# Attention and gated MLP on one core: batch 1 loaded in chunks, its k turned by DMA, and a new order for the opening

## The chip, the core and the metric

The kernel runs on one core of a Trainium2 chip. The metric is device time in microseconds (us): 309.43 us is the median of the three runs shown (308.65 to 309.45). A profile is one further execution in which every engine's instructions are recorded. A core has TensorE (PE), VectorE (DVE), ScalarE (ACT), GpSimd (POOL) and SyncE (SP), each with a queue of its own, and DMA queues that are fed here by POOL and SyncE.

## The reference

```python
B, H, S, D = 8, 8, 576, 64
scores = scale * np.matmul(q, k.transpose(0, 1, 3, 2))        # scale = 1/sqrt(D)
mask = (rel >= 0) & (rel < 64)                                # rel = row - column
attn = softmax(np.where(mask, scores, -1e9))
x = np.matmul(attn, v).transpose(0, 2, 1, 3).reshape(B * S, H * D)   # 4608 x 512
h = x @ w_in                                                  # 512 x 2048
out = (h * np.cos(h)) @ w_out                                 # 2048 x 512, float32
```

Inputs are float32. Each row of q attends to itself and the 63 rows before it.

## The kernel before, in words

**Attention.** A batch has eight heads, taken as four pairs p; a pair fills 128 partitions (2 x 64). The 576 rows are nine units j of 64 rows; a unit's 64 queries meet the 128 keys of units j - 1 and j. Scores are made in groups of up to four units, listed in `groups`; groups 0 to 7 are units 0 to 7 of batch 0 (group 2p + g is pair p, half g), group 8 is batch 0's last unit, groups 9 to 18 are batch 1. A group goes through `g_scores` (TensorE into a PSUM bank), `g_max` (DVE), `g_exp` (ACT), `g_inv` (DVE), `g_norm` (POOL or DVE, gives w), and `g_trans`, which transposes w by DMA, or on TensorE followed by `g_put` for the groups in `direct`. `values` and `values_half` multiply with v on TensorE, and `put_x` and `put_x_half` copy the result into xT. Odd units need a shifted copy of v, which the `spread_v` steps make.

**q and k.** Scores need q and k with the head dimension on partitions. In batches 0 and 1 `load_heads` (L161) loads a pair of heads in runs of nine rows, TensorE transposes them in 18 pieces of 64x64 per pair and tensor (`transposed`, L209), and `put_q` (L229) or `put_k` (L262) copy them out of PSUM into row order; the two heads of a pair are then multiplied one by one (L309), with lhsT of 64x64. Batches 2 and later use `load_chunk` (L178): 96 rows of all eight heads. Their k is turned by DMA transposes on SyncE (`turn_k`, L259); q is transposed on TensorE in six pieces of 96x128 per pair or turned by DMA, and `put_block` (L238) copies each head of a pair into its own half of a block that is zero elsewhere (`qblocks`), so that one product of 128x128 (L303) makes both heads' scores. `clear_first` (L545) zeroes those blocks.

**MLP.** Tokens go in tiles of 512. Tile 0 (batch 0's first 512 rows) is in the opening: `first_half` (L412; f = 0 to 7, half g) makes two columns of h for 256 tokens, `sine_half` and `gate_half` make the gate, and `second_part` (L431; quarter of d_ff, 128 tokens) sums the output. Tiles 1 to 8 run in the main loop (`first`, L450; L595, L598, L609), with the attention of later batches put between their products by planned times.

**The opening.** It is a hand-listed order, the string `FIRST` (L50 to L72): each word is a step that issues its instructions on its engines' queues at that place, and every engine works its own queue in order. The steps that matter here: `Lq`, `Lk`, `Lv`, `Lwi`, `Lwo` are loads of q, k, v, and quarters of w_in and w_out, nearly all of them on POOL's queue (pair 0 of batch 0 is loaded plain by SyncE and cast by `cq`, `ck`); `io` makes the iotas of the mask on POOL (L143), `mk` and `mc` the mask on DVE and ACT; `tq`, `pq`, `tk`, `pk` transpose and copy q and k of batch 0, `Tq`, `Pq`, `Tk`, `Pk` those of batch 1; `s m e i n w c` are the stages of groups 0 to 7 and `Gs Gm Ge Gi Gn Gw/Gc Gp` those of groups 8 to 18; `zA zB zC` and `yA yB y` spread v; `v x` are values of tile 0, `V X` of tile 1; `h S g` the halves of w_in products, sines and gates, `o oc` the w_out parts and their copies; `ms` are the clears; `tb`, `tb2` load ScalarE's tables. The letter at a step's end names its engine (a ACT, d DVE, p POOL, s SyncE). A load on POOL also waits, in turns of eight completion semaphores, for the load eight places before it.

Of the kernel before, what the change touches and what calls it, by code (L numbers as in the profile page):

```python
# [10 lines left out]
def _safe_warn(msg, *a, **kw):  # L11
# [64 lines left out]
def kernel(  # L76
# [32 lines left out]
    qtiles += [turned[:, p] for p in range(PAIRS)]  # L109
# [99 lines left out]
    def transposed(name, b, p):  # L209
        t_ps = ps_t.tile([128, S], BF16, tag="t", name=f"t{name}_ps")  # L210
        of = st[name, b]
        if b < 2:
            for c in range(RC):
                for h in range(2):
                    d = slice(64 * h, 64 * h + 64)
                    nc.tensor.transpose(t_ps[d, 64 * c:64 * c + 64], of[d, p, 64 * c:64 * c + 64], ident[d, d])
        else:
            for c in range(TURNED.get(b, 0) if name == "q" else 0, NC):
                nc.tensor.transpose(t_ps[:, NP * c:NP * c + NP], of[:, c, 128 * p:128 * p + 128], ident[:NP, :NP])  # L219
        return t_ps  # L220


    def in_order(t_ps, to, b):
        return (t_ps.rearrange("d (c p) -> d p c", c=RC), to.rearrange("d (p c) -> d p c", c=RC)) if b < 2 else (t_ps, to)

    def tr_q(b, p):
        st["tq", b, p] = transposed("q", b, p)

    def put_q(b, p, engine=None):  # L229
        of, to = in_order(st.pop(("tq", b, p)), qtiles[b * PAIRS + p], b)  # L230
        if b:
            copy(engine, to, of)
        elif engine == "a":
            nc.scalar.mul(to, of, scale)
        else:
            nc.vector.tensor_scalar(to, of, scale, None, ALU.mult)

    def put_block(b, p, h):  # L238
        d = slice(64 * h, 64 * h + 64)
        lo = TURNED.get(b, 0) * NP // 64  # L240
        copy("d", qblocks[(b % 2) * PAIRS + p][d, lo:, h], st["tq", b, p][d].rearrange("d (j t) -> d j t", j=NU)[:, lo:])
# [40 lines left out]
    def g_scores(n, which):  # L282
# [13 lines left out]
        for u, (b, p, j) in enumerate(units):  # L296
# [5 lines left out]
            if b > 1:  # L302
# [4 lines left out]
            for h in range(2):  # L307
                d = slice(64 * h, 64 * h + 64)
                nc.tensor.matmul(out=s_ps[d, u, 0:64 * chunks].rearrange("p (a t) -> p a t", a=chunks),  # L309
                                 lhsT=qtiles[b * PAIRS + p][d, 64 * j:64 * j + 64], rhs=rhs[d], start=n >= n_first,  # L310
# [237 lines left out]
    def spread_first(lo, hi):  # L548
# [5 lines left out]
             "Lq1": lambda p: load_heads("q", 1, p, 1), "Lk1": lambda p: load_heads("k", 1, p, 1),  # L554
# [4 lines left out]
             "tq": lambda p: tr_q(0, p), "tk": lambda p: tr_k(0, p), "Tq": lambda p: tr_q(1, p), "Tk": lambda p: tr_k(1, p),  # L559
             "pq": lambda p, engine: put_q(0, p, engine), "pk": lambda p, engine: put_k(0, p, engine),  # L560
             "Pq": lambda p, engine: put_q(1, p, engine), "Pk": lambda p, engine: put_k(1, p, engine),
# [87 lines left out]
```

## Time and profile before

| what | before |
|---|---|
| median of the runs shown | 309.43 us |
| span of the profiled execution | 306.3 us |
| DVE, ACT, POOL busy | 75%, 76%, 63% |
| HBM read, written | 36.70 MB, 9.44 MB |
| DMA packets | 159945, of which 148256 are under 512 B |

The span is from the first to the last instruction of the profiled execution; the runs' times are some 3 us longer. A row of a timeline gives start, duration, engine, line, operation, tiles and count; a row of a group gives its count, then busy time and mean ns of one, then the engine's idle time before it and what ended it. TensorE products are pipelined and their ends are modelled, so the time of one is read from start to start.

### The profile page before, as it was taken

The numbers are of one execution on the slowest core, as the hardware profiler recorded it, in microseconds if no ns is written. First come the engines' busy times: TensorE is split into PE (matmuls) and PEld (weight loads), VectorE is DVE, ScalarE is ACT, GpSimd is POOL, SyncE is SP. The second block draws the span as 40 slices with busy tenths as digits, with TensorE's granted clock in tenths as the row PEclk, the third lists the DMA queues.
The fourth block names the chain that finished last, engine by engine and source line by source line (L and its number), as shares of the span: only waits on it lengthen the run. The fifth ranks groups of instructions, "written<-read, shape, count | busy, mean of one in ns | idle before, by whom it ended". The sixth has DMA issues, their size and how long they took to land.

```text
span 306.3 us, 7904 instructions
## 1 busy us (share of the span) xinstructions
PE 296.2 (97%) x2616; PEld 159.0 (52%) x2616; DVE 228.5 (75%) x908; ACT 234.3 (76%) x785; POOL 192.5 (63%) x228
## 2 busy tenths in 40 slices
PE   3889999999999999999999999999999999999996
PEld 2768844545555555445544555454545554454443
DVE  5999978599769976798579857986698668235801
ACT  5998799677997799779976997699879986116600
POOL 8998579995659669967998599959903930000000
PEclk9999999999999999999999999999999999999999
DMA  7999999999999995999999999999794643011011
GB/s 146 179 212 192 200 180 130 121 149 191 226 113 116 175 223 80 121 133 232 125 121 137 231 143 104 157 221 148 86 137 107 169 78 141 2 68 71 1 67 70
DMA packets 159945, 42.14 MB, mean 138 GB/s; under 512 B 148256, under 2 KB 155168, under 8 KB 159904
## 3 DMA queue, kind: packets, MB, share of 16 engines
q0 software_dynamic: 100192, 18.06, 80.1%
q1 hardware_dynamic: 59568, 23.38, 40.6%
q8 instruction: 20, 0.33, 0.4%
q14 instruction: 21, 0.17, 0.2%
q10 hardware_dynamic: 144, 0.20, 0.2%
HBM read 36.70 MB, written 9.44 MB: 151 GB/s over the span
## 4 chain that ended last, share of the span: by engine, by line
PE 90%; POOL 4%; DMA 2%; DVE 1%; ACT 1%; issue 1%; POOLq 0%; DVEq 0%; ACTq 0%
PE h_ps L453 35%; PE out_ps L609 35%; PE h_ps L417 5%; PE s_ps L303 4%; PE out_ps L436 4%; PE o_ps L384 3%; DMA k<-in_k_dram 2%; POOL w L353 2%; PE tq_ps L219 1%; POOL v L188 1%; PE out_ps L465 1%; PE s_ps L309 1%; PE tw_ps L364 1%; POOL w_in L204 1%; ACT e L336 1%
## 5 line engine op out<-in xcount | busy, mean ns | idle before, releaser
L609 PE MATMUL out_ps<-w_out,gT 128*128 128x512 bf16 x496 | 117.3, 379 | 0.0
L453 PE MATMUL h_ps<-xT,w_in 128*128 128x512 bf16 x512 | 115.3, 379 | 0.3
L595 ACT ACTIVATE sin<-h_ps 128x512 f32<-128x512 f32 x128 | 73.7, 598 | 32.7 <-PE h_ps L453 31.4
L598 DVE TENSOR_TENSOR gT<-h_ps,sin 128x512 bf16<-128x512 f32 x128 | 82.1, 685 | 21.9 <-ACT sin L595 21.2
L336 ACT ACTIVATE e<-s,negm 128x128 f32<-128x128 f32 (+1 forms) x256 | 97.1, 382 | 0.6 <-DVE negm L324 0.6
L353 POOL TENSOR_TENSOR w<-e,rden 128x512 bf16<-128x512 f32 (+1 forms) x74 | 70.0, 962 | 36.6 <-DVE rden L346 18.8
L453 PEld LDWEIGHTS <-w_in 128*128 128x128 bf16 x512 | 48.8, 98 | 54.7 <-issue 0.4
L609 PEld LDWEIGHTS <-gT 128*128 128x128 bf16 x496 | 45.9, 98 | 44.2
L324 DVE CUSTOM_DVE_ANT_0 s<-s_ps,mask 128x128 f32<-128x128 f32 (+1 forms) x256 | 56.4, 279 | 1.7 <-PE s_ps L309 0.9
L336 ACT ACTIVATION_READ_ACCUMULATOR e<-s,negm 128x1 f32 x256 | 48.3, 189 | 0.0
L182 POOL DMA_DIRECT2D q<-in_q_dram x36 | 28.3, 785 | 10.7 <-DMA q<-in_q_dram 4.0
L188 POOL DMA_DIRECT2D v<-in_v_dram x40 | 34.4, 878 | 0.3 <-issue 0.2
L182 POOL DMA_DIRECT2D k<-in_k_dram x36 | 28.2, 783 | 3.9 <-DMA k<-in_k_dram 1.2
L137 ACT COPY out_sb<-out_ps 128x512 f32<-128x512 f32 (+1 forms) x18 | 10.2, 566 | 24.5 <-PE out_ps L609 18.4
L346 DVE RECIPROCAL rden<-den 128x4 f32<-128x4 f32 (+1 forms) x79 | 13.1, 166 | 19.0 <-ACT e L336 18.6
L303 PEld LDWEIGHTS <-qB 128*128 128x128 bf16 x216 | 16.5, 98 | 14.2
L137 DVE CAST xT<-o_ps 128x512 bf16<-128x512 f32 x24 | 15.5, 677 | 10.1 <-PE o_ps L384 10.1
L137 DVE COPY out_sb<-out_ps 128x512 f32<-128x512 f32 x18 | 12.4, 690 | 13.2 <-PE out_ps L609 12.5
L324 DVE DVE_READ_ACCUMULATOR2_ANT negm<- 128x1 f32 x256 | 21.3, 83 | 0.0
L303 PE MATMUL s_ps<-kT,qB 128*128 128x128 bf16 (+1 forms) x216 | 21.2, 216 | 0.0
L137 POOL COPY v<-v 64x1536 bf16<-64x1536 bf16 (+3 forms) x12 | 18.8, 1570 | 0.3
L137 DVE COPY qB<-tq_ps 64x384 bf16<-64x384 bf16 (+1 forms) x40 | 15.6, 390 | 0.4
(70 smaller groups left out, 257.8 us busy)
## 6 DMA issues: line engine op xcount, KB each, us to landing
out_dram<-out_sb SPq DMA_DIRECT2D x16, 512.0 KB, 7.5
v<-in_v_dram POOLq DMA_DIRECT2D x32, 128.0 KB, 5.7
q<-in_q_dram POOLq DMA_DIRECT2D x36, 96.0 KB, 8.6
k<-in_k_dram POOLq DMA_DIRECT2D x36, 96.0 KB, 8.5
w_in<-in_moe_w_in_dram POOLq DMA_DIRECT2D x4, 512.0 KB, 8.7
w_out<-in_moe_w_out_dram POOLq DMA_DIRECT2D x4, 512.0 KB, 10.8
wT<-w SPq DMA_TRANSPOSE x68, 4.4
q<-in_q_dram POOLq DMA_DIRECT2D x7, 144.0 KB, 6.0
```

Source lines behind the costliest of these rows:

```text
L137: {"a": nc.scalar.copy, "p": nc.gpsimd.tensor_copy}.get(engine, nc.vector.tensor_copy)(out, in_)
L182: nc.gpsimd.dma_start(out=st[name, b][:, c].rearrange("p (h d) -> p h d", h=H), in_=src.rearrange("h p d -> p h d"))
L188: nc.gpsimd.dma_start(out=vt.rearrange("p (h d) -> p h d", h=H), in_=v[b, :, c * 128:c * 128 + n, :].rearrange("h p d -> p h d"))
L303: nc.tensor.matmul(out=s_ps[:, u, 0:64 * chunks].rearrange("p (a t) -> p a t", a=chunks), lhsT=qblocks[(b % 2) * PAIRS + p][:, j].rearrang ...
L324: nc.vector.tensor_tensor_reduce(out=s[:, u, c], in0=s_ps[:, u, c], in1=mask[:, 2 - j % 2 if j else 0, c], scale=-scale if b else -1.0, sc ...
L336: nc.scalar.activation(e[:, u, c], s[:, u, c], AF.Exp, bias=negm[:, u:u + 1], scale=1.0 if n < n_first else -1.0, accum_out=den[:, u:u + 1])
L353: (nc.gpsimd if engine == "p" else nc.vector).tensor_tensor(out=w[:, 0:u], in0=e[:, 0:u], op=ALU.mult, in1=rden[:, 0:u].unsqueeze(2).to_br ...
L417: nc.tensor.matmul(out=h_ps[:, half * e:half * e + half], lhsT=w_in_sb[:, ks, ff * 128:ff * 128 + 128], rhs=st["xT", 0][:, ks, half * g:ha ...
L453: nc.tensor.matmul(out=st["h", ff], lhsT=w_in_sb[:, ks, ff * 128:ff * 128 + 128], rhs=st["xT", mt][:, ks], start=start, stop=stop)
L595: nc.scalar.activation(sin, h_ps, AF.Sin, bias=math.pi / 2.0)
L598: nc.vector.tensor_tensor(out=gt[:, e], in0=h_ps, in1=sin, op=ALU.mult)
L609: nc.tensor.matmul(out=o_ps[e], lhsT=gT[ff // 2][:, ff % 2, ms * 128:ms * 128 + 128], rhs=w_out_sb[:, ff], start=ff == 0, stop=ff == n_ff - 1)
```

## The change

Batch 1's q and k are loaded by `load_chunk`, in six chunks each, where `load_heads` loaded four pairs each. Its k is turned by six DMA transposes on SyncE (`Rk`); the steps `Tk` and `Pk` are gone. Its q is transposed on TensorE in six pieces of 96 rows per pair (`Tq`), and `Pq` copies each head with `put_block`, on DVE or ACT, into the zero-padded blocks of the second set. Scores of batch 1 are full-size products. The list `FIRST` is a new one from end to end; the places of the loads, cut to the POOL queue's order up to the last quarter of w_out, are

```
before: Lq0.1 Lk0.1 Lq0.2 Lk0.2 Lq0.3 Lk0.3 Lq1.0 Lk1.0 Lq1.1 Lk1.1 Lv0.0-3 Lwi.0 Lwi.1 Lwi.2
        (six n, with zB on SyncE) Lwi.3 (n) Lwo.0 Lq1.2 Lk1.2 Lq1.3 Lv1.0 Lwo.1 Lk1.3 Lwo.2 Lwo.3
after:  Lk0.3 Lq0.3 Lq0.2 Lq0.1 Lk1.0 Lv0.1 io Lk0.2 Lk0.1 Lv0.0 Lwi.0 Lv0.3 Lq1.5 Lwi.2 zA.1
        Lk1.3 Lwi.1 n.3.0 Lv0.2 Lk1.5 n.0.0 Lwi.3 n.3.1 Lq1.2 Lk1.1 Lq1.4 Lk1.2 Lq1.0 Lq1.3 Lq1.1
        Lk1.4 zB.0 Lv1.4 zC ms.6 ms.2 Lwo.0 Lwo.1 Lv1.0 Lwo.2 Lv1.3 Lv1.2 Lv1.1 Lwo.3
```

and TensorE's order from the first half tile of w_in on, in the new list, is

```
after:  h.0.0 h.0.1 h.0.3 w.2.1 h.0.4 w.1.1 w.0.1 h.0.2 h.0.6 h.0.7 v.0.1 v.1.1 h.0.5 h.1.0 h.1.1 h.1.6
        Tq.0 Tq.1 h.1.3 Tq.2 h.1.4 h.1.5 h.1.7 h.1.2 Gs.14 Gs.12 Tq.3 o.0.2 (quarter 0, tokens 2) ...
```

In the old list groups 9 to 12 of batch 1 have their scores ahead of the first h; in the new one they all stand behind the last.

```diff
@@ transposed, in_order, put_q, put_block @@
-        if b < 2:
+        if b == 0:
             for c in range(RC):
...
-        of, to = in_order(st.pop(("tq", b, p)), qtiles[b * PAIRS + p], b)
-        if b:
-            copy(engine, to, of)
-        elif engine == "a":
+        of, to = in_order(st.pop(("tq", b, p)), qtiles[p], b)
+        if engine == "a":
             nc.scalar.mul(to, of, scale)
...
-    def put_block(b, p, h):
+    def put_block(b, p, h, engine="d"):
         d = slice(64 * h, 64 * h + 64)
         lo = TURNED.get(b, 0) * NP // 64
-        copy("d", qblocks[(b % 2) * PAIRS + p][d, lo:, h], ...)
+        copy(engine, qblocks[(b % 2) * PAIRS + p][d, lo:, h], ...)
@@ g_scores @@
-            if b > 1:
+            if b:
                 nc.tensor.matmul(out=s_ps[:, u, 0:64 * chunks]..., lhsT=qblocks[(b % 2) * PAIRS + p][:, j]..., rhs=rhs,
...
@@ steps @@
-             "Lq1": lambda p: load_heads("q", 1, p, 1), "Lk1": lambda p: load_heads("k", 1, p, 1),
+             "Lq1": lambda c: load_chunk("q", 1, c), "Lk1": lambda c: load_chunk("k", 1, c),
...
-             "Pq": lambda p, engine: put_q(1, p, engine), "Pk": lambda p, engine: put_k(1, p, engine),
+             "Pq": lambda p, h, engine: put_block(1, p, h, engine), "Rk": lambda c: turn_k(1, c),
```

More of the change, by code (lines that the diff above doesn't have):

```diff
@@ L108 @@
     turned = const.tile([128, PAIRS, S], BF16, name="qT")
-    qtiles += [turned[:, p] for p in range(PAIRS)]
     qsets = [const.tile([128, PAIRS, NU, 2, 64], BF16, name=f"qB{i}") for i in range(2)]
@@ L223, in in_order @@
     def in_order(t_ps, to, b):
-        return (t_ps.rearrange("d (c p) -> d p c", c=RC), to.rearrange("d (p c) -> d p c", c=RC)) if b < 2 else (t_ps, to)
+        return (t_ps.rearrange("d (c p) -> d p c", c=RC), to.rearrange("d (p c) -> d p c", c=RC)) if b == 0 else (t_ps, to)
     def tr_q(b, p):
@@ L236, in put_q @@
             nc.vector.tensor_scalar(to, of, scale, None, ALU.mult)
-    def put_block(b, p, h):
+    def put_block(b, p, h, engine="d"):
         d = slice(64 * h, 64 * h + 64)
         lo = TURNED.get(b, 0) * NP // 64
-        copy("d", qblocks[(b % 2) * PAIRS + p][d, lo:, h], st["tq", b, p][d].rearrange("d (j t) -> d j t", j=NU)[:, lo:])
+        copy(engine, qblocks[(b % 2) * PAIRS + p][d, lo:, h], st["tq", b, p][d].rearrange("d (j t) -> d j t", j=NU)[:, lo:])
     def turn_q(b, c):
@@ L309, in g_scores @@
                 nc.tensor.matmul(out=s_ps[d, u, 0:64 * chunks].rearrange("p (a t) -> p a t", a=chunks),
-                                 lhsT=qtiles[b * PAIRS + p][d, 64 * j:64 * j + 64], rhs=rhs[d], start=n >= n_first,
+                                 lhsT=qtiles[p][d, 64 * j:64 * j + 64], rhs=rhs[d], start=n >= n_first,
                                  stop=n >= n_first or u == len(units) - 1, skip_group_check=True)
@@ L558 @@
              "io": put_steps, "mk": put_masks, "mc": cast_masks, "ms": clear_first,
-             "tq": lambda p: tr_q(0, p), "tk": lambda p: tr_k(0, p), "Tq": lambda p: tr_q(1, p), "Tk": lambda p: tr_k(1, p),
+             "tq": lambda p: tr_q(0, p), "tk": lambda p: tr_k(0, p), "Tq": lambda p: tr_q(1, p),
              "pq": lambda p, engine: put_q(0, p, engine), "pk": lambda p, engine: put_k(0, p, engine),
-             "Pq": lambda p, engine: put_q(1, p, engine), "Pk": lambda p, engine: put_k(1, p, engine),
+             "Pq": lambda p, h, engine: put_block(1, p, h, engine), "Rk": lambda c: turn_k(1, c),
              "zA": spread_first(0, 1), "zB": spread_first(1, 3), "zC": lambda engine: spread_v(0, 1, engine, 3, 4),
```

42 rows, old and new, of the table FIRST are left out of this document.

## The prediction

> **What bounds the kernel now.** I read the page's first two parts first, then a table by stages, then each engine's instructions in order of time. The page's head:
>
> ```profile
> span 306.3 us, 7904 instructions
> PE 296.2 (97%) x2616; PEld 159.0 (52%) x2616; DVE 228.5 (75%) x908; ACT 234.3 (76%) x785; POOL 192.5 (63%) x228
> PE   3889999999999999999999999999999999999996
> DMA  7999999999999995999999999999794643011011
> ```
>
> TensorE is full from the fifth slice on; only the first 30 us have slack, and DMA is loaded there from the start. Busy time of each engine by stage:
>
> ```profile
> core 0: us, PE busy (x) PEld busy (x) DVE busy (x) ACT busy (x) POOL busy (x), PEclk, DMA share, GB/s
> 4.00:18.65 14.65, 11.90 (x323) 9.40 (x324) 12.33 (x26) 12.14 (x54) 13.34 (x19) 1.00 1.44 174
> 18.65:21.18 2.53, 2.53 (x63) 2.08 (x63) 2.47 (x15) 2.53 (x14) 2.06 (x3) 1.00 1.24 209
> 21.18:57.17 35.99, 35.77 (x434) 23.40 (x432) 31.19 (x118) 30.21 (x107) 29.01 (x36) 1.00 1.45 172
> 57.17:306.25 249.08, 245.97 (x1804) 124.09 (x1800) 180.13 (x743) 187.09 (x611) 144.80 (x162) 1.00 1.18 130
> ```
>
> The borders are two marks on TensorE: H at 21.18 us, the first product of the opening's w_in half tiles, and E at 57.17 us, the first product of token tile 1. Behind E the list of TensorE work is the same in both kernels, so what the change is worth is how far E moves. Between H and E TensorE is idle 0.22 us of 35.99.
>
> ```profile
> 21.18 1.93 PE L417 MATMUL h_ps<-xT,w_in 128*128 128x256 bf16 x16
> ...
> 36.67 0.47 PE L216 MATMUL tk_ps<-ident,k 64*64 64x64 bf16 x18
> 36.97 0.73 PE L216 MATMUL tq_ps<-ident,q 64*64 64x64 bf16 x36
> 37.64 1.04 PE L436 MATMUL out_ps<-w_out,gT 128*128 128x512 bf16 x4
> ...
> 39.98 0.55 PE L309 MATMUL s_ps<-kT,qT 64*64 64x128 bf16 x14
> 40.46 1.90 PE L436 MATMUL out_ps<-w_out,gT 128*128 128x512 bf16 x8
> ```
>
> What sets H is ScalarE: 28 exponentials of batch 0 with hardly a pause, then the copy of x.
>
> ```profile
> L336 ACT ACTIVATE e<-s_ps,negm 128x128 f32<-128x128 f32 x28 | 10.0, 409 | 0.4 <-DVE negm L319 0.3
> ...
> 8.18 0.36 ACT L336 ACTIVATE e<-s_ps,negm 128x128 f32<-128x128 f32 x1
> 8.52 0.37 ACT L336 ACTIVATE e<-s_ps,negm 128x128 f32<-128x128 f32 x1
> ...
> 20.16 1.21 ACT L137 CAST xT<-o_ps 128x512 bf16<-128x512 f32 x2
> ```
>
> **Term 1, H: +0.2 us.** The new list puts the two iotas of the mask (L143) behind four loads of heads, a chunk and a v on POOL.
>
> ```profile
> 1.27 0.53 POOL L143 IOTA mask<- 64x128 f32 x2
> 1.75 0.75 POOL L165 DMA_DIRECT2D q<-in_q_dram  x1
> 4.25 0.55 POOL L165 DMA_DIRECT2D q<-in_q_dram  x1
> 37.92 0.79 POOL L182 DMA_DIRECT2D q<-in_q_dram  x1 [1.86 <-PE tq_ps L216]
> 8.69 3.52 POOL L188 DMA_DIRECT2D v<-in_v_dram  x4 [0.21 <-issue]
> 2.03 0.23 DVE L147 TENSOR_TENSOR mask<-mask 128x128 f32<-128x128 f32 x1
> 2.97 0.11 DVE L151 MEMSET mask<- 128x64 f32 x1
> ```
>
> Four heads take 4.25 - 1.75 = 2.50, the chunk 0.79, the v 3.52 / 4 = 0.88: the iotas go from 1.27 to 5.4. With 0.53 for them and 1.05 for the mask on DVE (2.03 to 3.08) it is 7.05; then on DVE put_q of pair 0, put_k of pair 3, two half clears and the first maximum. I estimate these five from the kernel's own: two copies near 0.7 each, two clears near 0.5, a maximum 0.7, together 3.1. So the first exponential starts near 10.15, not 8.18. In front of x, ScalarE then has 28 exponentials at 8.52 - 8.18 = 0.34 (9.6) and one put_q (0.65), where before it had that put_q, another, and two k copies. Half a microsecond of pauses and copy later, 10.15 + 9.6 + 0.65 + 0.3 + 0.6 = 21.3 to 21.4. I take +0.2; bounds -0.3 (no pauses) and +0.5.
>
> The TensorE work taken from ahead of H (72 transposes, four groups of scores with 14 blocks) is 72 x 0.018 + 14 x 0.069 = 2.3 us by the rates of the next term. **It is worth nothing**, because ScalarE covers it. If that cover were gone, H could come up to 2.3 us sooner.
>
> **Term 2, TensorE's work between H and E: +0.2 us.** By starts in the fence above, 54 of the 64x64 transposes take 37.64 - 36.67 = 0.97 (0.018 each), and 14 half-height scores 0.48, so a block of two is 0.069. The two new forms already stand in later batches:
>
> ```profile
> 59.77 0.42 PE L219 MATMUL tq_ps<-ident,q 96*128 96x96 bf16 x6
> 60.03 0.38 PE L453 MATMUL h_ps<-xT,w_in 128*128 128x512 bf16 x1
> ...
> 72.45 0.20 PE s_ps L303 x4
> ```
>
> Six transposes of a chunk take 60.03 - 59.77 = 0.26, four full blocks 0.20. Removed: 72 transposes 1.30 and 26 blocks 1.79. Added: 24 chunk transposes 1.04, 36 full blocks 1.80, the filler product that comes to stand behind H 0.2, four more transposes of w 0.2. Net +0.15. The 128 products of w_in and 64 of w_out stay.
>
> **Term 3, w_in arrives late for H: +1.1 us.** POOL's loads are served in the order of their issue. Rates while heads move (8 to 11 us), while v does (13.2 to 15.2) and while w_in does (17 to 20), then latencies of heads, w_in and w_out:
>
> ```profile
> DMA packets 555, 0.57 MB, mean 189 GB/s; under 512 B 62, under 2 KB 555, under 8 KB 555
> DMA packets 2449, 0.31 MB, mean 154 GB/s; under 512 B 2449, under 2 KB 2449, under 8 KB 2449
> DMA packets 609, 0.62 MB, mean 208 GB/s; under 512 B 16, under 2 KB 608, under 8 KB 608
> DMA to landing us min/median/max: 4.7/5.7/6.3
> DMA to landing us min/median/max: 6.4/8.7/12.3
> DMA to landing us min/median/max: 7.5/10.8/11.9
> ...
> 12.18 2.27 POOL L204 DMA_DIRECT2D w_in<-in_moe_w_in_dram  x3
> ...
> 31.91 0.74 POOL L207 DMA_DIRECT2D w_out<-in_moe_w_out_dram  x1 [2.40 <-DMA w_out<-in_moe_w_out_dram]
> ```
>
> Heads (147 KB) need 0.75, v (131 KB) 0.85, a chunk (98 KB, written in the same small pieces as v) 0.64 by v's rate. A quarter of w_in (524 KB) needs 2.5 by its rate; the third of the three that were issued from 12.18 lands near 13.7 + 12.3 = 26, which asks for 2.8. In the new order six heads (4.5), four v (3.4), four chunks (2.6) and all w_in (11.2) end with the last quarter: 21.7 us. The first load is issued at 1.3 and lands 4.7 later, of which 0.75 is its service; with about 0.5 for the plain loads beside it, 1.3 + 4.7 - 0.75 + 0.5 + 21.7 = 27.4. The same count for before's third quarter (issued from 1.75; ten heads, four v, three quarters) gives 6.2 + 19.3 = 25.5, half a microsecond short of that 26; with half of this added the last quarter is due at 27.65. TensorE asks for this quarter after five half tiles (8 x 0.11 each) and three transposes of w (0.7), at 21.4 + 5.1 = 26.5. It waits 1.1; bounds 0 (w_in at 2.5, chunks at heads' rate) and 2.0.
>
> A rule speaks against these chunks. The Trainium skill, "DMA: Bandwidth & Descriptors", in its opening table, wants at least 512 B in a transfer for line rate and has smaller ones do a read-modify-write. Taken as half rate, an estimate from that page, a chunk would be 1.0 us and the term 1.4 larger; v's row, with pieces as small, shows 154 against 189 GB/s, so the row decides for 0.64.
>
> **Term 4, the order behind it on POOL: +0.3 us.** The last k chunk (L182) waits, by the eight semaphores that loads take in turn, for that last quarter of w_in; behind it on POOL stand the spread of v (zB.0) that the second half's values need, then zC, two clears, and all of w_out.
>
> ```profile
> 47.03 1.03 POOL L137 COPY v<-v 64x1024 bf16<-64x1024 bf16 x1
> ```
>
> 27.65 + 0.3 + 0.8 + 1.03 = 29.75 for the spread, where TensorE arrives at 27.65 + 2 x 0.88 = 29.4: 0.3, bounds 0 and 1.
>
> **Term 5, k turned by DMA, and w_out: +0.7 us.** Twelve chunks and six transposes pass the DMA engines before w_out, where eight heads did, four of them behind w_in. Latencies of transposes of k between 120 and 134 us, and of w between 42 and 60 us:
>
> ```profile
> DMA to landing us min/median/max: 2.4/8.0/8.7
> DMA to landing us min/median/max: 3.1/5.8/7.0
> ```
>
> The last chunk lands near 27.65 + 8 x 0.64 + 1.3 for two transposes of 98 KB = 34.1; its transpose needs 2.4 us alone and about 7 among loads, so 36.5 to 41.1, and TensorE wants it at 29.75 + 0.8 (values) + 9 x 0.88 + 0.8 (chunk transposes) = 39.3. The queue is nearly empty then, for w_out is issued only at 29.75 + 0.7 + 1.0 + two clears of about 1 us = 33.5, so I take 0.2 of a possible 0 to 1.8. The quarters of w_out land at 33.5 + 6.4 (the lowest of w_in's latencies) = 39.9, then, at 2.7 each with the v's between, at 42.6, 46.2 and 51.5; TensorE wants them at about 40.2, 43.2, 46.4 and 51.5. All four are just in time, where before the last was there by 31.91 + 11.9 = 43.8. For so many margins of 0.3 us I add 0.5; bounds 0 and 2.5.
>
> Costed at nothing: the eight block copies of q on DVE and ScalarE (in the shade of w_in products), the six transposes' 1.3 us each on SyncE (nothing queued behind them until w's own), clears moved to POOL (counted in 33.5).
>
> **Sum.** 0.2 + 0.2 + 1.1 + 0.3 + 0.7 = **+2.5 us**: E at 59.7 and the profiled span 306.3 + 2.5 = 308.8. The median of the shown runs, 309.43, is 3.2 above that execution's span; I put the shift on the median: **311.9 us**.
>
> **Rivals.** (A) Transposes among loads: the last one of k takes 7, not 2.4. It decides from a latency of 39.3 - 34.1 = 5.2 on. Then TensorE waits 1.8 there, and four transposes' service (0.64 each) stands ahead of w_out, whose last quarter comes 2.6 later. Where only w_out is late it is 2.5 - 0.7 + 2.6 = +4.4, 313.8; with both, +6.2, 315.6. For it: the medians of 8.0 and 5.8 above. Against it: 2.4 in an empty queue. On two rings the Trainium skill ("DMA: Bandwidth & Descriptors", "Queues, rings and completion order") has each DMA engine go round between them packet by packet; by that no transpose would wait 7 us behind loads, and A would be out. The medians above disagree.
> (B) The loads are in time: w_in at 2.5 a quarter and chunks at heads' rate (0.52) bring the last quarter to 25.8, before 26.5, and the rest with it; only terms 1 and 2 stay: +0.4, 309.8. For it: the 208 GB/s row. Against it: the 26 for the third quarter.
> (C) The other side, faster: the exponentials start below 9.2, at 8.5 say, and the last quarter of w_in lands by 24.8. Then H falls to 19.7, E follows 36.0 + 0.2 behind it at 55.9: -1.3, 308.1. It decides only where both come true; of the 2.3 us taken from ahead of H it is what ScalarE would let through. For it: ScalarE has one put_q and two k copies less ahead of x. Against it: the iotas' new place, and B's rates still leave the quarter 1.0 late.
>
> **Chances.** Forecast 0.50, A 0.20, B 0.20, C 0.10. A measurement of this kernel can tell about 0.3% (0.9 us) from none: below 308.5 is faster, up to 310.4 the same. C gives faster 0.08 and same 0.02, B faster 0.02, same 0.12 and slower 0.06, the forecast same 0.03. So faster 0.10, same 0.17, slower 0.73. Range 308.7 to 315.2: it leaves out most of C and what lies in B below it (0.10) and the far half of A (0.08). The forecast's own range is 310.4 to 313.4.
>
> **What would show it.** H within 20.9 to 21.7 and ScalarE's exponentials from about 10; a gap on TensorE of about 1 us before the sixth half tile, released by the w_in load; first w_out products near 40; E at 59 to 61, and nothing gained or lost behind it. Terms 3 to 5 are wrong if TensorE has no gap over 0.3 us between H and E; the whole is wrong if H moves by over 1 us or E's shift is not the span's.

## The result: 321.1 us, 3.75% slower, and the profile after

The changed kernel takes 321.08 us (median of six runs, 319.59 to 321.81); the kernel before took 309.35 beside it. The ratio is 1.0375, 95% interval 1.0346 to 1.0403. The forecast was 311.9 and its range ended at 315.2: right in sign, 9.2 us short. One execution of all those behind the figures below, 320.25 us in run 9, counts as a slow one and is left out. The profiled execution spans 319.0 us, 12.7 more than before. The head of its page:

```profile
span 319.0 us, 7566 instructions
PE 295.9 (93%) x2428; PEld 159.9 (50%) x2460; DVE 229.4 (72%) x910; ACT 235.7 (74%) x788; POOL 194.8 (61%) x230
PE   2878939969999999999999999999999999999995
PEclk9999969979999999999999999999999999999999
DMA  8999999999993999499999999999694834011011
```

TensorE was full from the fifth slice on; now the sixth and the ninth slice have holes, and the granted clock, which before was full everywhere, dips in just these two (each slice is 8.0 us). TensorE is busy as long as before (295.9 against 296.2) although it has less to do, because some of its work now runs at a lower clock. The marks H and E of the prediction, and products on the way, in TensorE's order of time after the change:

```profile
21.50 3.03 PE L414 MATMUL h_ps<-xT,w_in 128*128 128x256 bf16 x24
...
39.49 0.28 PE L300 MATMUL s_ps<-kT,qB 128*128 128x128 bf16 x2
44.65 0.26 PE L300 MATMUL s_ps<-kT,qB 128*128 128x128 bf16 x1 [4.89 <-DMA kT<-k]
...
45.94 0.63 PE L433 MATMUL out_ps<-w_out,gT 128*128 128x512 bf16 x1
...
50.25 0.36 PE L300 MATMUL s_ps<-kT,qB 128*128 128x64 bf16 x4
...
66.05 0.74 PE L381 MATMUL o_ps<-wT,v 128*64 128x64 bf16 x22 [2.51 <-DMA wT<-w]
```

H is at 21.50 (21.18 before), E at 69.54 (57.17 before). First the waits of TensorE that the profile lists between the two (us in total, times, longest), then rows of a table by stages, of which the last begins at E. Behind the length, a row gives the busy time of PE, PEld, DVE, ACT and POOL with their counts, then the granted clock, the DMA share and GB/s:

```profile
PE s_ps L300 <- DMA kT<-k: 4.9, 1, 4.9
PE o_ps L381 <- DMA wT<-w: 2.5, 1, 2.5
PE o_ps L400 <- POOL v L136: 0.7, 1, 0.7
PE h_ps L414 <- DMA w_in<-in_moe_w_in_dram: 0.6, 1, 0.6
PE out_ps L433 <- issue: 0.6, 2, 0.3
```

```profile
44.65:52.00 7.35, 7.13 (x40) 3.88 (x41) 4.70 (x31) 5.04 (x26) 1.45 (x2) 0.70 1.66 189
...
66.05:69.54 3.49, 3.16 (x58) 1.98 (x58) 0.00 (x0) 1.07 (x2) 3.49 (x4) 0.52 2.58 149
69.54:319.00 249.46, 244.30 (x1775) 124.21 (x1800) 178.28 (x733) 186.88 (x605) 141.75 (x158) 1.00 1.16 128
```

From E to the end it is 249.46 us against 249.08: nothing is lost there, so 12.4 of the 12.7 us arise ahead of E. Two stretches run at a clock of 0.70 and 0.52, each right behind one of the two long waits. Both waits are for DMA transposes; the chain of waits names them (start, us, what):

```profile
34.56 10.04 DMA kT<-k
...
59.72 6.28 DMA wT<-w
```

The transpose of k's chunk 4, the last of six, was under way 10.04 us. It was issued right behind the first two quarters of w_out, which POOL issued from 33.49 on:

```profile
33.49 1.52 POOL L206 DMA_DIRECT2D w_out<-in_moe_w_out_dram  x2
```

### The profile page after: what moved, and what is told of

The parts are those of the page before. It is cut to its first block, busy times and chain, and to the rows that moved or that the text cites. A ratio compares the mean times of both kernels' runs of the same rounds, so it can differ in the third digit from the quotient of the medians.

```text
span 319.0 us, 7566 instructions
## 1 busy us (share of the span) xinstructions
PE 295.9 (93%) x2428; PEld 159.9 (50%) x2460; DVE 229.4 (72%) x910; ACT 235.7 (74%) x788; POOL 194.8 (61%) x230
## 4 chain that ended last, share of the span: by engine, by line
PE 71%; DMA 10%; DVE 6%; POOL 5%; ACT 4%; issue 2%; SPq 1%; POOLq 0%; DVEq 0%
PE h_ps L450 30%; PE out_ps L606 29%; PE s_ps L300 4%; DMA wT<-w 3%; DMA kT<-k 3%; DVE gT L595 3%; PE out_ps L433 3%; PE o_ps L381 3%; ACT e L333 3%; DMA k<-in_k_dram 2%; DMA v<-in_v_dram 2%; SPq L257 1%; PE tq_ps L218 1%; PE out_ps L462 1%; DVE qB L136 1%
## 5 line engine op out<-in xcount | busy, mean ns | idle before, releaser
L606 PE MATMUL out_ps<-w_out,gT 128*128 128x512 bf16 x482 | 114.7, 379 | 0.8 <-issue 0.2
L350 POOL TENSOR_TENSOR w<-e,rden 128x512 bf16<-128x512 f32 (+1 forms) x68 | 64.3, 961 | 44.5 <-DVE rden L343 37.8
L181 POOL DMA_DIRECT2D k<-in_k_dram x42 | 32.9, 784 | 9.4 <-DMA k<-in_k_dram 2.9
L181 POOL DMA_DIRECT2D q<-in_q_dram x42 | 33.0, 786 | 5.9 <-DMA q<-in_q_dram 2.4
L300 PE MATMUL s_ps<-kT,qB 128*128 128x128 bf16 (+1 forms) x252 | 25.2, 219 | 4.9 <-DMA kT<-k 4.9
L300 PEld LDWEIGHTS <-qB 128*128 128x128 bf16 x252 | 19.4, 99 | 16.2 <-issue 0.8
L343 DVE RECIPROCAL rden<-den 128x4 f32<-128x4 f32 (+1 forms) x79 | 12.7, 164 | 17.3 <-ACT e L333 17.0
L136 POOL COPY v<-v 64x1536 bf16<-64x1536 bf16 (+3 forms) x14 | 19.6, 1401 | 1.9 <-DMA v<-in_v_dram 1.5
L136 DVE COPY qB<-tq_ps 64x384 bf16<-64x384 bf16 (+1 forms) x45 | 17.8, 396 | 0.5
```

Source lines behind the costliest of these rows:

```text
L136: {"a": nc.scalar.copy, "p": nc.gpsimd.tensor_copy}.get(engine, nc.vector.tensor_copy)(out, in_)
L181: nc.gpsimd.dma_start(out=st[name, b][:, c].rearrange("p (h d) -> p h d", h=H), in_=src.rearrange("h p d -> p h d"))
L300: nc.tensor.matmul(out=s_ps[:, u, 0:64 * chunks].rearrange("p (a t) -> p a t", a=chunks), lhsT=qblocks[(b % 2) * PAIRS + p][:, j].rearrang ...
L343: nc.vector.reciprocal(out=rden[:, 0:len(groups[n])], in_=den[:, 0:len(groups[n])])
L350: (nc.gpsimd if engine == "p" else nc.vector).tensor_tensor(out=w[:, 0:u], in0=e[:, 0:u], op=ALU.mult, in1=rden[:, 0:u].unsqueeze(2).to_br ...
L606: nc.tensor.matmul(out=o_ps[e], lhsT=gT[ff // 2][:, ff % 2, ms * 128:ms * 128 + 128], rhs=w_out_sb[:, ff], start=ff == 0, stop=ff == n_ff - 1)
```

## The experiments

Two theories at first. **Theory 1:** single DMA transposes that come out among loads, and the clock that falls while TensorE waits for them. **Theory 2:** the chunks are simply too much for the DMA engines ahead of w_out; whatever comes last is late. Later the question was what is left once the k transpose is mended. All runs but the sixth and the tenth start from the changed kernel. H and E are read from the profiled execution of each, in us; times are medians, ratios are those of the mean times to the kernel before on the same chip. Runs 1 to 4, 5 to 10, 11 and 12, and 13 and 14 were on four different chips, so across these groups the ratios compare better than the times; the kernel before took 308.7 to 309.6 on them.

| run | H | E | E to end | time | ratio, 95% interval |
|---|---|---|---|---|---|
| before | 21.18 | 57.17 | 249.1 | 309.35 | |
| changed kernel | 21.50 | 69.54 | 249.5 | 321.08 | 1.0375 (1.0346 to 1.0403) |
| 1 k's chunk 4 early | 22.17 | 63.71 | 249.6 | 314.71 | 1.0164 (1.0121 to 1.0207) |
| 2 w_out behind the k transpose | 22.10 | 69.78 | 249.4 | 321.01 | one run |
| 3 products in the wait for k | 21.36 | 67.67 | 249.7 | 319.55 | 1.0333 (1.0290 to 1.0376) |
| 4 k turned on TensorE | 22.37 | 65.09 | 250.4 | 316.77 | 1.0222 (1.0183 to 1.0261) |
| 5 run 1, batch 2's loads apart | 22.52 | 63.41 | 251.9 | 317.08 | 1.0272 (1.0254 to 1.0289) |
| 6 before, with full-size blocks alone | 25.02 | 62.37 | 249.2 | 313.74 | 1.0175 (1.0156 to 1.0194) |
| 7 run 5, q and the spread of v moved | 21.56 | 62.04 | 253.9 | 317.41 | 1.0275 (1.0249 to 1.0301) |
| 8 run 1, batch 2's loads behind w | 22.19 | 60.16 | 255.0 | 317.85 | 1.0265 (1.0201 to 1.0330) |
| 9 run 8, q and the spread of v moved | 22.46 | 61.23 | 256.3 | 318.85 | 1.0261 (1.0176 to 1.0347) |
| 10 before, with four groups' scores late | 22.71 | 61.03 | 249.8 | 311.61 | 1.0069 (1.0037 to 1.0101) |
| 11 run 1, products in its pauses | 21.72 | 62.32 | 249.2 | 314.40 | 1.0209 (1.0172 to 1.0247) |
| 12 run 1, two groups' w on TensorE | 21.41 | 60.71 | 249.6 | 312.72 | 1.0126 (1.0105 to 1.0148) |
| 13 run 12, further waits mended | 21.52 | 60.34 | 248.9 | 311.28 | 1.0074 (1.0048 to 1.0101) |
| 14 run 13, products ahead of H | 21.45 | 60.04 | 249.0 | 310.90 | 1.0061 (1.0035 to 1.0086) |

### 1. k's chunk 4 early

```diff
-  n.3.1.p Lq1.2 Lk1.1 Lq1.4 ... Lk1.2 Rk.2 ... Lq1.1 Lk1.4 zB.0.p ... Rk.0 ... g.1.7 Rk.4 Gs.14.3
+  n.3.1.p Lk1.4 Lk1.1 Lq1.4 ... Lk1.2 Rk.4 Rk.2 ... Lq1.1 Lq1.2 zB.0.p ... Rk.0 ... g.1.7 Gs.14.3
```

> Chunk 4 of k changes places with chunk 2 of q on POOL, and its transpose goes third on SyncE, ahead of the ones of chunks 2, 1 and 0; nothing else moves. Theory 1 (the changed kernel lost its time because the last transpose of k went out behind the first two quarters of w_out and so took 10.0 us, and then the granted clock fell): this transpose is issued near 28.3 and lands before 36, TensorE's 4.89 us at 44.65 are gone, the clock behind them stays at 1.00, and w_out's second quarter decides instead (0.3 to 1.3 us). E comes 4.5 to 8.5 us sooner, the time is 312.5 to 316.5. Theory 2 (the DMA engines simply have too much to move ahead of w_out; whichever transfer comes last is late): the wait moves to q's chunk or to w_out and keeps over 3 us, and the time stays above 318.

The wait for kT is gone, and 6.4 us with it. w_out held nothing up, where 0.3 to 1.3 us were expected. The transpose that is last now, of chunk 0, was issued 0.5 us behind w_out's first quarter and took 7.6 us, but nothing waited for it. The rest of TensorE's long waits, in its order of time:

```profile
34.34 0.22 PE L217 MATMUL tq_ps<-ident,q 96*128 96x96 bf16 x1 [0.43 <-DMA q<-in_q_dram]
35.29 0.60 PE L217 MATMUL tq_ps<-ident,q 96*128 96x96 bf16 x10 [0.74 <-DMA q<-in_q_dram]
...
58.21 0.32 PE L380 MATMUL o_ps<-wT,v 128*64 128x64 bf16 x8 [0.97 <-DMA wT<-w]
60.25 0.72 PE L380 MATMUL o_ps<-wT,v 128*64 128x64 bf16 x22 [1.72 <-DMA wT<-w]
```

Theory 1 stands for the largest part; theory 2 asked for a time above 318. What it says of a transfer that takes the last place is true on a small scale: the q chunk that now comes last costs 1.17 us.

### 2. w_out behind the k transpose

```diff
-  zC.p ms.6.p ms.2.p Tq.2 Pq.2.0.a Pq.2.1.d Lwo.0 ... Rk.4
+  zC.p ms.6.p ms.2.p Tq.2 Pq.2.0.a Pq.2.1.d ... Rk.4 wt Lwo.0
+  wt: nc.gpsimd.tensor_copy(late, k_tile(1)[:, 0, LAST:LAST + 1])
```

> The first quarter of w_out, and with it all that POOL issues later, waits for the last transpose of k (a one-element copy of its result on POOL stands ahead of it). Theory 1 (transposes share the DMA engines with w_out's quarters): alone the transpose lands 2.4 to 4 us after its issue at 34.6, by 38.5, before TensorE wants it at 39.5; now w_out is late: its first quarter lands near 44 and TensorE waits about 4 us for that, so the time is 319 to 323. Rival (the transpose is slow because five others stand ahead of it on SyncE's queue): it still takes about 10 us, w_out comes 10 us later, and the time is above 326.

The DMA queues between 36.6 and 37.7, where the last k transpose is under way, and then TensorE's row where it waits:

```profile
q1 hardware_dynamic: 416, 0.10, 45.2%
issues: line engine op xcount, KB each, median us to landing
kT<-k SPq DMA_TRANSPOSE x1, 2.4
```

```profile
44.04 1.89 PE L432 MATMUL out_ps<-w_out,gT 128*128 128x512 bf16 x4 [2.92 <-DMA w_out<-in_moe_w_out_dram]
```

The same transpose, last in SyncE's row as before, takes 2.4 us in place of 10.04 once w_out stands behind it. SyncE's queue is not what was slow. The wait only changes its name: w_out is now late, the values of token tile 1 wait 3.17 us for wT, and the time is that of the changed kernel.

### 3. Products in the wait for k

```diff
+        for _ in range(20 if n == 14 else 0):
+            nc.tensor.matmul(out=s_ps, lhsT=ident, rhs=mask16[:, 0:4]..., start=True, stop=True, ...)
```

> Twenty products of 128x512 of constants stand on TensorE in front of the product that waits 4.89 us for the last k transpose; at 0.216 each they fill 4.3 us of the wait and are needed by nothing. Theory 1 (the wait costs twice: itself, and a lower granted clock, 0.70 over the next 7.35 us): the wait shrinks to about 0.6, the clock from 44.65 to 52 is 1.00, and E comes 1.5 to 2.5 us sooner; the time is 318.5 to 320. Rival (the slow stretch has another cause, such as data that TensorE reads just after it landed): the stretch stays at 0.70, and the time is 321 or more.

TensorE's order of time:

```profile
39.45 4.48 PE L283 MATMUL s_ps<-mask,ident 128*128 128x512 bf16 x20
...
44.77 0.22 PE L303 MATMUL s_ps<-kT,qB 128*128 128x128 bf16 x1 [0.74 <-DMA kT<-k]
...
48.23 0.36 PE L303 MATMUL s_ps<-kT,qB 128*128 128x64 bf16 x4
```

From the product that waited to the four narrow scores it takes 48.23 - 44.77 = 3.46 us; the same work took 50.25 - 44.65 = 5.60 in the changed kernel. The half clock cost 2.1 us beside the wait, and products that nobody needs give it back: E is 1.9 sooner. The median of the times is 1.5 lower, but the intervals of the ratios overlap, so the gain is shown in the profile alone.

### 4. k turned on TensorE

```diff
-  Rk.0 ... Rk.5
+  Tk.2 Pk.2.d Tk.1 Pk.1.a Tk.0 Pk.0.d (among the last half tiles) ... Tk.3 Pk.3.d (among w_out's products)
```

> The same loads and list, but k of batch 1 is turned on TensorE like q (24 transposes of a chunk, four copies of 128x576 on DVE and ScalarE), and SyncE's six DMA transposes are gone. Theory 1 (k turned by DMA is what failed): no wait for kT, 1.04 us more of TensorE work, w_out's quarters 2 to 4 us earlier, E near 63.4 instead of 69.5; the time is 313 to 317. Theory 2 (too much to move ahead of w_out, whoever turns k): w_out's first product still waits over 2 us, and the time is above 318.

No wait for kT, w_out in time, and 4.3 us won: theory 1 again. But E is at 65.09 and not at 63.4, for the second wait has grown:

```profile
58.26 0.32 PE L380 MATMUL o_ps<-wT,v 128*64 128x64 bf16 x8 [0.51 <-DMA wT<-w]
61.54 0.80 PE L380 MATMUL o_ps<-wT,v 128*64 128x64 bf16 x22 [2.96 <-DMA wT<-w]
```

### 5, 7. Batch 2's loads apart from w's transposes

```diff
-  Lq2.0 Lv0.4 Lq2.4 ... Lq2.5 Lq2.2 Lq2.3 ... Lq2.1 ... Lk2.0 ... Lk2.4 Lk2.2 Lk2.3 Lk2.5 ... Lk2.1
+  Lq2.0 Lv0.4 Lq2.4 Lq2.5 Lq2.2 Lq2.3 Lq2.1 ... wt(w of group 10) Lk2.0 Lk2.4 Lk2.2 Lk2.3 Lk2.5 Lk2.1
```

> The run with chunk 4 of k early, and in addition the loads of batch 2 kept away from the six DMA transposes of w that token tile 1 waits for: its four q chunks go out on POOL before these transposes, its six k chunks behind the landing of the transpose of group 10 (a one-element copy on POOL waits for it). Theory 1 (these transposes take 4.4 to 6.7 us because chunk loads share the DMA engines, where 2.3 were enough alone): they land in under 4 us, TensorE's waits of 0.97 and 1.72 us at 58.2 and 60.3 are gone, the granted clock behind them is 1.00 and not 0.75, E comes 2.7 to 3.9 us sooner than 63.7; the time is 310.8 to 312.3. Theory 2 (all ten groups of batch 1 have their softmax behind the last half tile, ScalarE is busy 16.44 of 16.67 us there, and w is ready too late whatever the loads do): the waits keep at least 1.5 us of their 2.7, and the time is 313.5 or more.

The time lies in theory 2's range, but neither theory came true as written. The last three transposes did fall to 2.8 to 3.5 us, and no value waited for them. But the four q chunks now stood on POOL ahead of the normalizations of w, so w itself came late: TensorE waited 2.47 us for a w ahead of 57.46, the clock fell again, and later the scores of batch 2 waited 1.8 us for their kT. Run 7 puts the spread of v on DVE and two transposes of q one half tile later. It fails in the same places: 2.69 us of wait for w, 1.60 and 1.22 for batch 2's kT (E to end 253.9), and q's transposes still wait, 1.08 and 0.77. What was expected of it:

> All that the other runs point to, on the changed kernel: chunk 4 of k early, batch 2's loads apart from w's transposes, the first two transposes of q behind one more half tile (they waited 0.43 and 0.74 us for the last q chunk), and the spread of v for the second half on DVE instead of POOL (0.72 us of wait). If waits and the clock behind them are the whole of the loss, E is at 57.5 to 59.0 and the time 308.5 to 310.5. If something else is lost in the opening, it stays above 311.

### 8, 9. Batch 2's loads behind w, nothing ahead of the normalizations

```diff
-  Lq2.5 Lq2.2 Lq2.3 ... Lq2.1 ... Lk2.0 ... Gp.8.a Lk2.4 Lk2.2 Lk2.3 Lk2.5 ... Lk2.1
+  Gp.8.a wt(w of group 10) Lq2.5 Lq2.2 Lq2.3 Lq2.1 Lk2.0 Lk2.4 Lk2.2 Lk2.3 Lk2.5 Lk2.1
```

> As the run with chunk 4 of k early, and all ten loads of batch 2 that were issued from 51.7 on go out only when the transpose of group 10 has landed; nothing stands in front of the normalizations on POOL this time. Theory 1 (w's transposes lose their time to chunk loads): they are issued from 48.2 to 55.5 as there, and the last four land 2.4 to 4 us after their issue where they took 6.1 to 6.7; token tile 1's values start near 57 without a wait over 0.3 us, E comes 2.7 to 3.9 us sooner than 63.7 and the time is 310.8 to 312.3, unless batch 2's chunks, now 3 to 4 us later, hold its transposes of q near 63 (then up to 2 us are lost again). Theory 2 (the softmax of ten groups behind the last half tile is too long for the work that covers it): the waits keep 1.5 us or more, and the time is 313.5 or more.

The first half of theory 1 is confirmed: of w's six transposes the last three take 3.7, 2.7 and 3.4 us, the values start at 57.59 without a wait, and E is at 60.16, 3.6 sooner than in run 1. The second half failed: E to end is 5.5 us longer. TensorE's rows of batch 2's first scores:

```profile
76.54 0.20 PE L299 MATMUL s_ps<-kT,qB 128*128 128x64 bf16 x1 [0.68 <-DMA kT<-k]
78.21 0.27 PE L299 MATMUL s_ps<-kT,qB 128*128 128x128 bf16 x2 [1.46 <-DMA kT<-k]
79.56 0.27 PE L299 MATMUL s_ps<-kT,qB 128*128 128x128 bf16 x1 [1.07 <-DMA kT<-k]
```

3.2 us of waits, now for batch 2's k transposes, and a granted clock of 0.50 from 79 to 82.5. Run 9 moved the transposes of q and the spread of v as well and gained nothing: the first scores waited 0.54 and 0.89 us, for a block of q and for the gate that frees their bank, and later ones 4.1 us for kT.

> As the run before it, with the first three transposes of q two to four half tiles later and the spread of v for the second half on DVE. Those took 1.17 us of waits for the last q chunk, and 0.7 for the spread. If waits are the loss, E comes another 1 to 2 us sooner and the time is 309 to 311; if q's blocks then come late for the first scores, it stays where the run before it is.

### 6. Full-size blocks alone, on the kernel before

```diff
-            if b > 1:
+            if b:                      # full-size products on zero-padded q
-                            in_=src.rearrange("(a h) (p c) d -> (h p) a (c d)", h=2, c=RC))
+        for h in range(2): ... in_=src[h].rearrange("(c p) d -> p c d", c=RC)      # batch 1
-  "Pq": put_q(1, p, engine)
+  "Pq": put_block(1, p, 0), put_block(1, p, 1)
```

> The kernel before, its list and its pairs of heads kept, with one part of the change alone: full-size score products on zero-padded q for batch 1. To have the tokens in order its heads are loaded in rows of 64 (two loads for a pair of heads, in pieces as small as a chunk's), and q is copied head by head; k is still turned on TensorE. TensorE saves 36 blocks x 0.019 = 0.7 us. If loads by pairs are what kept the kernel before full, it stays full: TensorE idles under 1 us between H and E, and the time is 308.3 to 310.5. If small pieces and more copies are enough to do the harm (eight more issues on POOL of 0.77 each, 1.6 us more on the DMA engines, eight copies of 0.63 instead of four of 0.65), w_in or the scores are late and the time is above 311.5.

4.9 us slower. H is at 25.02: ahead of it TensorE waits 3.70 us for a w of batch 0. Its normalization stands on POOL behind eight issues of some 0.75 us, where the kernel before has four of 0.55. The first normalizations on POOL, in this run and in the kernel before:

```profile
17.80 4.08 POOL L357 TENSOR_TENSOR w<-e,rden 128x512 bf16<-128x512 f32 x4
```

```profile
14.51 6.13 POOL L353 TENSOR_TENSOR w<-e,rden 128x512 bf16<-128x512 f32 x6
```

They begin 3.3 us later. From H to E it is another 1.4 us more, with waits for w_out (0.84), w_in (0.45), w (0.44) and k (0.26), where the kernel before waits 0.22 in all. What feeds the full-size products is what costs here, issues on a queue that has other work.

### 10. Four groups' scores late, on the kernel before

```diff
-  Tk.1 n.1.0.p s.2.1.1 Pq.1.d Gs.10.2 m.2.1 Gs.9.4 ... Gs.12.0 ... Gm.10 ... Gs.11.2 Gm.9 Gm.12 ... Gm.11
+  tb2 Tk.2 Lv1.3 Pk.2.d Gs.10.2 Gs.9.3 Gm.10 Gm.9 Ge.10 ... Ge.9 Gs.12.0 Gm.12 Ge.12 ... Gs.11.2 Gm.11 Ge.11
```

> The kernel before with one part of the new order alone: the scores and maxima of groups 9 to 12 of batch 1, which stand ahead of the first half tile, move behind the last one, as in the changed kernel; loads, forms and everything else stay. My forecast counted this as 1.0 us of products (14 blocks x 0.069) that ScalarE had covered and now are not: the time is 309.5 to 311. If the chain from these scores to the values of token tile 1 is what is too long, the transposes of w come 2 us or more later, TensorE waits for them, and the time is 311.5 to 314.

2.2 us slower. The time, 311.6, is at the lower end of what the second expectation gave, but not for its reason: TensorE waits for no transpose of w. Its rows, in order of time:

```profile
22.71 1.92 PE L416 MATMUL h_ps<-xT,w_in 128*128 128x256 bf16 x16
...
44.32 1.90 PE L435 MATMUL out_ps<-w_out,gT 128*128 128x512 bf16 x8 [0.78 <-DVE negm L323]
...
61.03 1.25 PE L452 MATMUL h_ps<-xT,w_in 128*128 128x512 bf16 x5
```

H to E is 38.32 against 35.99: the 1.0 us of products that nothing covers now, 0.78 for a maximum, and about half a microsecond that no long wait shows. The transposes of w are issued 2.8 to 3.8 us later, but no value waits for them. What was not expected is H, 1.5 later with less work ahead of it: TensorE waits 1.36 us there for a w, and from 19 to 22 us the granted clock is 0.50 in this profile. That is not so in every execution: the five with a mean clock of 0.994 or 0.995 took 311.5 to 313.2 us, the five with 1.000 took 310.8 to 311.7, so part of the 2.2 us is the clock.

### 11, 12. The two remedies for run 1

```diff
+  11: transposes of the identity into tw_ps (10, 8, 8) ahead of three transposes of w; 5 and 18 products of constants into o_ps
+  12: DIRECT = (0, 1, 2, 7, 8);  Gc.9 -> Gw.9 ... Gp.9.d;  Gc.10 -> Gw.10 ... Gp.10.d
```

> The run with chunk 4 of k early, and products of constants in TensorE's other pauses: 8 to 10 transposes of the identity ahead of the three transposes of w that waited 0.83, 0.50 and 0.53 us before H (the granted clock fell to 0.50 from 19.5 to 22.6 there), and 5 and 18 products into the output that waited 0.97 and 1.72 us for w at 58.2 and 60.3 (0.50 from 60.5 to 63.8). Nothing needs them and no wait goes away. If half of each spell at half clock is lost, that is 3.1 / 2 = 1.5 and 3.3 / 2 = 1.6 us: H back at 21.4 to 21.6, E 2 to 3 us sooner than 63.7, the time 311.5 to 313. If the spells cost nothing because other engines set the pace there, it stays at 314 to 315.5.

The clock is 1.00 throughout in the profile, H is at 21.72 and E 1.4 sooner, but the median of the times fell by only 0.3, the ratio is higher than run 1's, and the intervals overlap: a gain in time is not shown. Its four executions with a mean clock of 1.000 took 313.3 to 314.5 us, the two with 0.995 took 316.4 and 317.4. The products fill a wait and don't shorten it.

> The run with chunk 4 of k early, and the w of groups 9 and 10, which token tile 1's first values waited for, are turned on TensorE (eight transposes, some 0.45 us, and two copies on DVE) instead of by DMA; no load moves. If DMA transposes among loads are what is left of the loss, the waits of 0.97 and 1.72 us and the half clock behind them go, a wait of about 1 us for group 13's transpose takes their place at the last of the four values, E comes 2 to 3 us sooner than 63.7, and nothing is lost later: the time is 311.7 to 313. If w itself comes too late (ScalarE, DVE and POOL), TensorE waits for these w instead, and the time is 314 or more.

The waits of 0.97 and 1.72 us are gone, the clock is 1.00 throughout, E is 3.0 sooner, and nothing is lost later (E to end 249.6), as theory 1 had it. The time, 312.72, lies in its range; it is 2.0 below run 1, but on another chip, and by the ratios the gain is 1.2 us with intervals that overlap. One wait for a DMA transpose is left, that of group 13:

```profile
60.37 0.41 PE L380 MATMUL o_ps<-wT,v 128*64 128x64 bf16 x14 [1.34 <-DMA wT<-w]
```

### 13, 14. What is left

```diff
+  13: DIRECT = (0, 1, 2, 5, 7, 8), Gw.13 and Gp.13.d;  zB.0.p -> zB.0.d;  Tq.2 Tq.1 behind h.1.4, Tq.0 behind h.1.5
+  14: 13, and the transposes of the identity of run 11 ahead of H
```

> The run with w of groups 9 and 10 turned on TensorE, and in addition w of group 13 turned there, the spread of v for the second half on DVE instead of POOL, and q's first three transposes behind two or three more half tiles (pair 2 and 1 first). If the waits left are the whole of what is lost, 1.34 + 0.72 + 0.61 - 0.2 for four more transposes = 2.4 us come back: E 58.2 instead of 60.7, the time 309.6 to 311. If something that no wait shows is lost, or a new wait takes their place, it stays at 311.5 to 313.

> The run before it with 8 to 10 transposes of the identity in each of three pauses of TensorE ahead of H. If the pauses cost through the clock in some executions (0.50 from 19.5 to 22.6 in some of the profiles), its times scatter less and their median is 0.3 to 1 us lower; else it is the same within 0.4 us.

Run 13 is 311.28, just above its range for "waits are all". Its waits between H and E are for DVE, POOL, w_in and q, none over 0.81 us, 2.6 in all. With 0.3 for H and 0.7 for twelve more transposes on TensorE this is 3.6, more than the 3.2 us by which its E is late, so by this count nothing hidden is left. The stages from the last half tile on, of run 13 and of the kernel before:

```profile
39.50:58.00 18.50, 16.70 (x117) 8.49 (x116) 17.59 (x102) 18.35 (x86) 12.75 (x17) 1.00 1.81 168
```

```profile
36.67:57.17 20.50, 20.28 (x264) 10.06 (x264) 16.81 (x75) 17.68 (x79) 16.86 (x20) 1.00 1.59 151
```

ScalarE is busy 18.35 of 18.50 us in run 13 (17.68 of 20.50 before) and DVE 17.59 (16.81): with all ten groups of batch 1 behind the last half tile, their softmax is as long as TensorE's work there. Run 14 is 0.4 lower, its mean clock 0.999 to 1.000 in all ten executions where run 13 had 0.989 to 1.000, but the intervals overlap, and its times scatter as widely (1.8 us). Within run 13 the three executions at 0.989 took 312.1 to 312.6 us, the other eight 310.8 to 312.0. No version beat the kernel before.

## Why the prediction was wrong, by its own steps

**The failed step is the first half of term 5:** "The queue is nearly empty then, for w_out is issued only at 29.75 + 0.7 + 1.0 + two clears of about 1 us = 33.5, so I take 0.2 of a possible 0 to 1.8." The two times were right: the last chunk landed at 34.21 (34.1 forecast) and w_out was issued at 33.49. The conclusion was not: two quarters of w_out stood ahead of the transpose, the first by one microsecond. TensorE waited 4.89 us, not 0.2, and more than the 1.8 that I had as the upper bound, since 7 us from the rows of later batches is no bound for a transpose behind 1 MB of w_out. Run 2 shows the 2.4 us that I had counted, in the empty queue that I had assumed. Run 1 has the other half: with that chunk loaded and turned earlier, the wait is gone. This is rival A's mechanism, which got 0.20 and too low a price.

**Missing altogether: what a wait does to the clock.** Every price in the sum took a wait as its own length. Run 3 shows 2.1 us more behind this one. Behind the second wait it is about 1.3: from the product that waited to E the changed kernel takes 3.49 us, and run 8, at full clock, 2.2 for the same products (57.59 to 60.16, less 0.25 for ten products that stood ahead of the wait and 0.16 for a wait of its own).

**Missing too: w's transposes.** The sum has no term for them. But with groups 9 to 12 scored behind the last half tile, and all of them 5 us late, the transposes of w began at 54.52 (42.59 before) and so fell among batch 2's loads; 6.28 us for the one that counted, a wait of 2.51. The diff showed the order; I costed the moved products (term 2) and not the chain behind them.

The other terms, with the same marks:

| step | forecast | measured |
|---|---|---|
| H | +0.2 (exponentials from 10.15) | +0.32 (from 10.27) |
| TensorE's work H to E | +0.2 | about -0.1, as the rest of the sum |
| w_in's last quarter | lands 27.65, wait 1.1 | lands 27.52, wait 0.63 |
| spread of v on POOL | 0.3 | 0.72 |
| last k transpose | 0.2 | 4.89, and 2.1 of half clock |
| w_out just in time | 0.5 | hidden by the wait for k |
| w's transposes | none | 2.51, and 1.3 of half clock |
| sum: shift of E | +2.5 | +12.4 |

Terms 1 to 4 add up to 1.8 forecast and 1.6 measured; the whole miss lies in the last part. "Worth nothing" for the 2.3 us of TensorE work taken from ahead of H held in this profile, in part by luck: in the profiles of runs 1 and 10, with as little to do there, TensorE runs at half clock ahead of H, and H is at 22.2 and 22.7. The last section shows what decides between the two.

The rule of the Trainium skill that I set against rival A ("DMA: Bandwidth & Descriptors", "Queues, rings and completion order", turns between the rings packet by packet) I had read as one small packet against one. The DMA queues of the changed kernel from 38.6 to 44.5, while the k transpose was under way, say otherwise:

```profile
q0 software_dynamic: 1584, 0.79, 179.9%
q1 hardware_dynamic: 416, 0.10, 15.5%
```

The 416 packets of the transpose passed beside 1584 of POOL's ring, about one to four, in 5.9 us. The Trainium skill's packet there is typically a run of some 9 to 17 descriptors. Whether the profile counts such a run as one packet, no run here shows, so the rule as it is written may hold; my reading of it, by which rival A was out, does not.

## What to carry to other kernels

A small transfer that TensorE needs must be issued before the large ones that it doesn't need yet; a transpose issued one microsecond behind w_out took 10 us, and 2.4 with w_out held back until it had landed. Price a new wait on TensorE with the clock behind it, and where work is moved to a later place, follow its whole chain, down to the transfer at its end and what that will meet there. Loading by rows makes everything of a batch ready at once and late, where loading by pairs let four groups be scored early: here the later scores alone cost some 2 us (run 10), so such a form needs something else that covers that time.

## What the runs showed of the hardware

**The clock falls by half, in spells of one or two equal lengths.** The changed kernel by stages, cut near the places where the granted clock changes:

```profile
39.55:42.25 2.70, 0.21 (x3) 0.09 (x2) 0.80 (x2) 2.08 (x3) 1.28 (x2) 1.00 1.22 183
42.25:49.00 6.75, 4.13 (x20) 2.35 (x21) 3.66 (x22) 3.72 (x19) 1.45 (x2) 0.50 2.24 158
49.00:65.50 16.50, 14.43 (x102) 7.21 (x101) 13.83 (x80) 12.75 (x64) 11.79 (x15) 1.00 1.25 121
66.00:69.50 3.50, 3.12 (x57) 1.97 (x57) 0.00 (x0) 1.07 (x2) 3.50 (x4) 0.52 2.57 149
```

TensorE stands from 39.76; the clock is halved 2.5 us later and stays so for 6.8 us, 4.4 of them after work is back. The spell at 66 lasts about 3.4. Three short pauses with products between them are enough too, as in run 1:

```profile
17.85 0.40 PE L360 MATMUL tw_ps<-ident,w 128*128 128x128 bf16 x4 [0.83 <-DVE w L349]
18.74 0.40 PE L360 MATMUL tw_ps<-ident,w 128*128 128x128 bf16 x4 [0.50 <-POOL w L349]
19.67 0.61 PE L360 MATMUL tw_ps<-ident,w 128*128 128x128 bf16 x4 [0.53 <-DVE w L349]
```

There the clock was 0.50 from 19.5 to 22.9. Pauses of 0.76, 0.62 and 0.40 at the same place in the changed kernel left it at 1.00, and so did 0.83, 0.49 and 0.53 in run 13. A wait of 2.47 us for w in run 5 brought the clock down, one of 2.69 us in run 7 did not. So the length of a pause does not decide by itself.

What decides in these profiles is how busy TensorE is within one stretch of a fixed grid. In each of the eleven profiles in which the clock falls (the changed kernel and runs 1 to 10), all its changes lie whole multiples of 3.41 us apart: at 42.27, 49.09, 66.17 and 69.58 in the changed kernel, at 19.45, 22.86, 60.41 and 63.83 in run 1. Cut on that grid, TensorE is busy 13 to 57% of the stretch ahead of each of the 19 falls. All other stretches at full clock that begin later than 5 us have 56% or more, so the border here is near 57%. The stretch ahead of run 1's first fall, and the two in which the same pauses lie in the changed kernel:

```profile
16.04:19.45 3.41, 1.77 (x26) 1.06 (x23) 3.34 (x8) 3.41 (x21) 3.39 (x4) 1.00 1.47 197
...
14.97:18.38 3.41, 2.21 (x36) 1.32 (x30) 3.34 (x9) 3.41 (x23) 3.39 (x4) 1.00 1.58 192
18.38:21.79 3.41, 2.65 (x55) 1.99 (x56) 3.41 (x9) 3.25 (x18) 3.39 (x5) 1.00 1.52 195
```

That is 52% against 65 and 78%. Run 7's wait lies in two stretches, with 57 and 64%; run 5's lies in one, with 33%. The grid begins at another place in each profile, so a kernel meets it by chance. Laid at any place from 5 to 100 us, a stretch of 3.41 us has at least 62% in the profile of the kernel before and 57% in run 14's, but only 45% in run 13's. That fits the mean clocks: 1.000 in nearly all executions of the kernel before and of run 14, 0.989 to 1.000 in run 13's.

The Trainium skill ("TensorE: Matmul & The Clock Gate", "The HAM clock gate") has a free-running window of 3.41 us and half rate after an idle one. The grid and the spells of one and two windows agree; that the window must be idle does not, for none of the 19 stretches was. The Trainium skill's rule of thumb for pauses on the same page ("HAM oscillation", none over some 3.4 us) is too mild for this kernel, as the 2.51 us and run 1's three pauses show.

**A DMA transpose's time is set by its company:** 2.4 us alone (k in run 2), 2.8 to 4.2 behind a few chunk loads (the last four of w in run 5), 6.1 to 6.7 among chunk loads (the last three of w in run 1), 7.6 and 10.04 behind w_out (the last of k in run 1 and in the changed kernel).
